# A chunked recurrence with a feed-forward layer: score and state-read products of 64 rows in the two halves of TensorE

## The chip, the cores and the metric

The kernel runs on one core of one Trainium2 chip. The metric is the time of one execution on the device in microseconds (us); the time before is the median of three runs. A core has five engines that run beside each other, each with an instruction queue of its own: TensorE (PE) for matrix products, with a weight load of its own (PEld), VectorE (DVE), ScalarE (ACT), GpSimd (POOL) and SyncE (SP), which in this kernel issues all DMAs. Products land in PSUM, which has banks of 128 partitions x 512 float32; everything else lies in SBUF.

## What is computed

Four sequences (`batch`), 8 heads, 768 tokens, head size D = 32, state size N = 16. For every sequence and head a decaying state of 16 x 32 is carried over the tokens; its output, transposed to tokens x 256, goes through a layer 256 -> 2048 -> 256 with a softplus between.

```python
# per batch and head, chunk by chunk (the kernel takes 128 tokens at a time)
M = (C @ B.T) * decay(i, j)            # "scores", causal
y = M @ x + (C @ state) * decay_to_i   # inside the chunk + "state read"
state = decay_full * state + (B * decay_from_j).T @ x
...
h = y_all @ w_in                       # 3072 x 256 @ 256 x 2048
out = softplus(h) @ w_out              # @ 2048 x 256
```

## The kernel before

**Units.** A unit is 128 tokens of one sequence with all 8 heads: 24 units, 6 to a sequence. Units 0 to 11 (`i < FIRST`) come with C already laid apart by the host; units 12 to 23 come stacked and are made ready on the chip by `split_unit`. The feed-forward layer runs over 6 blocks of 512 tokens (4 units each) and 16 slices of 128 of the inner 2048: `first(j, k)` makes 6 matmuls into a bank `hp`, `parts_of` the softplus and its two roundings (`e`, `gh`, `gl`), `second(j, k)` 6 matmuls into the sums `acc0`, `acc1`. Every factor is split in a high and a low part of type float32r, hence three products for each one. A matmul of plain float32 shows as two instructions in the profile, one of float32r as one.

**Scores.** `score(i, g)` fills one bank `sp` with 4 heads x 128 x 128 (g = 0, 1 for the two groups of four heads). For units under 12 it is one float32 product of 64 rows and 512 columns per group; the two groups lie in rows 0 to 63 and 64 to 127, so each uses one half of the array. From unit 12 on it is two float32r products of 128 rows and 256 columns per group, against `c_rows`, a tile [128, 4, 2, 128] in which the C of two heads is laid apart: rows 0 to 63 of copy e = 0, rows 64 to 127 of copy e = 1, zeros elsewhere. `split_unit` makes the rounded parts of B (`b_rows`) and C (`c_all` for odd units; for even ones the first 512 columns of the constants' tile `kept`, free by then) on ACT and DVE, and two DMAs copy the halves of C into `c_rows`. The word `zero` at the start of the order clears `c_rows` once on POOL. `weigh` multiplies a bank of scores with the decays `rm` on DVE.

**Values and state reads.** Up to unit 7 a unit is read on its own (`read`, `within`, `grow`, `rest`). From unit 8 on units go in pairs. `pair_values(i)` (i even) makes the state products of both units into a bank `zp` (32 columns of the array at a time), the values of both units into one bank `yp` (again 32 columns at a time), and then the state read of unit i into the same bank: `read_into(i, yp)`, two float32 products of 128 rows, 128 columns and 128 tokens, with `tb` (the state spread by `spread`, times a mask `bd` that leaves each head its own rows) and `cc` (scaled C). A unit with i % 6 = 0 has no read. `pair_ends(i)` reads unit i + 1 into that bank, makes `y` = `yp` x `gg` in one DVE instruction of 512 columns, and rounds it to the layer's input (`xh`, `xl`).

**Order.** PE always keeps the order in which the program issues (line 132). Up to step 30 of the layer everything keeps an order written out by hand (`ORDER`, lines 53 to 70); from step 31 (`PINNED`) DVE, ACT and POOL are placed by the scheduler's own cost model. In the main loop a step is `second` of four steps ago, `first`, and then what is planned for it (lines 867 to 875): unit i has its scores in step s = 30 + 4 (i - 12), and for odd i the pair's values in s + 2 and its end in s + 3. So scores stand alone between 6 matmuls `hp` and 6 matmuls `acc`; the read of an odd unit does too; that of an even unit follows the values. Banks of PSUM with the tag `ps` are a ring of six: `hp`, `sp`, `zp` and `yp` take the next in turn, which must have been read out.

Of the kernel before, what the change touches and what calls it, by code (L numbers as in the profile page):

```python
# [10 lines left out]
F32 = mybir.dt.float32  # L11
F32R = mybir.dt.float32r
# [3 lines left out]
ALU = mybir.AluOpType  # L16
PSUM = bass.MemoryType.PSUM

P = 128
NB, NH, S, D, N = 4, 8, 768, 32, 16  # L20
SUB = 32
NC = P // SUB
NU = S // P
NQ = NH // 2
# [4 lines left out]
HEAD = 4  # L29
FIRST = 12  # L30
# [4 lines left out]
U_S = U_C + P  # L35
U_END = U_S + 2 * NQ * P
F_END = U_S + P + NQ * P
# [8 lines left out]
C_SEL = C_BD + NH  # L46
C_GB = C_SEL + P
C_OWN = C_GB + 4
C_END = C_OWN + 2 * NU * (NC + 1)

ORDER = """
zero la warm11 kc un2 hc1 hc0 hc2 un0 logr loga un1 logr loga w2 growth gb hc3 ft0 growth un3 gq0 ft0 w1 B2 D0 un5 fr0
gq0 gq2 fr0 D1 w0 S0 gq2 w7 B0 S1 M0 un6 B1 M0 U0 fr0 M1 D2 I0 fr0 U0 gd M1 C1 S2 T1 un4 D3 W2 G0 un7 U1 C2 M2 U2 R1
B3 G0 W2 ft2 M2 C3 X0 D5 U1 W1 W2 U3 ft2 I1 fr2 warm3 U2 T2 fr2 S5 G1 T3 G1 U3 W2 R2 T4 S3 W2 w3 M5 X1 M5 I2 gg3 W2 R3
D4 M3 fr2 W0 warm6 B4 C4 M3 fr2 U4 C5 W0 warm1 D7 S4 G2 U4 gg6 W0 G2 I3 T5 S6 W0 M4 W0 R5 X2 R4 M4 C7 I5 w4 W0 D6 I4
# [16 lines left out]
LAG = 4  # L74
WRAW = 4
EARLY = 8


def constants():

    k = np.arange(P)
    ch = k // SUB
    upto = (k[:, None] <= k[None, :]).astype(np.float32)
    mid = np.stack([(ch < c) + 0.5 * (ch == c) for c in range(NC)], 1).astype(np.float32)
    out = np.zeros((P, K_END + C_END), np.float32)
    mats = [(mid[:, c : c + 1] - upto) * (ch <= c)[None, :] for c in range(NC)] + [1.0 - upto]
    for i, m in enumerate(mats):
        out[:, i * P : (i + 1) * P] = m
    out[:, C_V : C_V + NC] = mid
    out[:, C_V + NC] = 1.0  # L90
    sel = out[:, K_END:]
    sel[:, C_BD : C_BD + NH] = k[:, None] // N == np.arange(NH)[None, :]
    part = (k // N) % 4
    gb = part >= 2
    gc = part % 2 == 1
    sel[:, C_GB + 0] = gb
    sel[:, C_GB + 1] = 1.0 - 2.0 * gb
    sel[:, C_GB + 2] = gc
    sel[:, C_GB + 3] = 1.0 - 2.0 * gc
    sel[:, C_SEL:C_GB] = (k % NH)[:, None] == (k // N)[None, :]  # L100
    sel[:, C_OWN:] = (k // NH)[:, None] == (np.arange(2 * NU * (NC + 1)) // (NC + 1))[None, :]
    return out


# [1 line left out]
def recurrence_then_ffn(ctx: ExitStack, tc: tile.TileContext, fst, un, alr, w_in, w_out, const, outT):  # L106
# [25 lines left out]
    PE = InOrder(nc.tensor, True)  # L132
# [3 lines left out]
    def load(out, in_):  # L136

        tc.keep_in_program_order(nc.sync.dma_start(out, in_))  # L138
# [107 lines left out]
            gg_s[i + v] = gg[:, :, v * P : v * P + P]  # L246


    c_rows = cp.tile([P, NQ, 2, P], F32R, name="c_rows")

    def split_unit(i):
        if i < FIRST:
            return
        t = bc_s[i]
        b_rows = p2.tile([P, NQ, P], F32R, tag="b_rows", name=f"b_rows{i}")

        def split(out, j):
            raw = t[:, j * NQ * P : (j + 1) * NQ * P].rearrange("p (q t) -> p q t", q=NQ)
            g, be = (kb[:, C_GB + v : C_GB + v + 1] for v in (2 * j, 2 * j + 1))
            A.activation(out, raw, AF.Copy, scale=be)  # L260
            V.scalar_tensor_tensor(out, raw, g, out.bitcast(F32), op0=ALU.mult, op1=ALU.add)

        if i % 2:
            c_all = p2.tile([P, NQ, P], F32R, tag="c_all", name=f"c_all{i}", bufs=1)
        else:
            c_all = kept[:, : NQ * P].bitcast(F32R).rearrange("p (q t) -> p q t", q=NQ)
        split(c_all, 1)
        for e in range(2):
            rows = slice(64 * e, 64 * e + 64)
            load(c_rows[rows, :, e].bitcast(F32), c_all[rows].bitcast(F32))  # L270
        split(b_rows, 0)
        st[i] = b_rows

    some = p2.tile([P, 512], F32, tag="o0", name="some", bufs=1)[:, :16].bitcast(BF16)

# [73 lines left out]
        return xparts[j], t0 - starts[j]  # L349

    bd = kb[:, C_BD : C_BD + NH]
    state = {}

    mid = defaultdict(dict)

    def decays(i):

        b, u = divmod(i, NU)
        fc = f_tok[b][1]
        rm = p2.tile([P, NH, NC, SUB], F32, tag="rm", name=f"rm{i}")  # L360
        Pl.affine_select(  # L361
            out=rm.rearrange("p h c i -> p (h c) i"),
            in_=fc[:, u].rearrange("p h c -> p (h c)").unsqueeze(2).broadcast_to([P, NH * NC, SUB]),
            pattern=[[0, NH], [SUB, NC], [1, SUB]],
            compare_op=ALU.is_ge,
            fill=0.0,
            base=0,
            channel_multiplier=-1,
        )
        mid[i]["rm"] = rm  # L370
# [24 lines left out]

    def score(i, g):
        sp = mid[i]["sp", g] = ps.tile([P, 512], F32, tag="ps", name=f"sp{i}_{g}")
        if i < FIRST:
            rows = slice(64 * g, 64 * g + 64)
            if i < HEAD:  # L400
                t = head_in["l"][rows, i]
                PE.matmul(sp, t[:, :P], t[:, P:], start=True, stop=True)
                return
            PE.matmul(sp, un_s[i][rows, U_S : U_S + P], un_s[i][rows, U_S + P : F_END], start=True, stop=True)
            return
        b_rows = st[i]
        for v in range(2):
            q = 2 * g + v
            PE.matmul(
                sp[:, 2 * v * P : 2 * (v + 1) * P],  # L410
                b_rows[:, q],
                c_rows[:, q].rearrange("p e t -> p (e t)"),
                start=True,
                stop=True,
            )

    def weigh(i, g):
        if g == 0:
# [31 lines left out]
    def spread(i):  # L450

        if i % NU > 0:
            tb = mid[i]["tb"] = p2.tile([P, NQ, 2, D], F32, tag="tb", name=f"tb{i}", bufs=3)
            V.tensor_tensor(
                tb,
                state[i - 1].rearrange("p (e d) -> p e d", d=D).unsqueeze(1).broadcast_to([P, NQ, 2, D]),
                bd.rearrange("p (q e) -> p q e", e=2).unsqueeze(3).broadcast_to([P, NQ, 2, D]),
                op=ALU.mult,
            )

# [41 lines left out]

    def attend_scores(i):
        decays(i)
        for g in range(2):
            score(i, g)
            weigh(i, g)
        scale_b(i)
        scale_c(i)
# [14 lines left out]
    def read_into(i, yp):  # L524
        if i % NU > 0:
            for g in range(2):
                PE.matmul(
                    yp[:, g, i % 2],
                    mid[i]["tb"][:, 2 * g : 2 * g + 2].rearrange("p q e d -> p (q e d)"),
                    mid[i]["cc"].rearrange("p c i -> p (c i)"),  # L530
                    start=False,
                    stop=True,
                    skip_group_check=True,
                )

    def pair_values(i):

        zp = ps.tile([P, 512], F32, tag="ps", name=f"zp{i}")
        for v in range(2):
            if (i + v) % NU < NU - 1:  # L540
                bp = mid[i + v]["bp"]
                for q in range(NQ):
                    PE.matmul(
                        zp[32 * q : 32 * q + 32, 2 * v * D : 2 * (v + 1) * D],
                        bp[:, 2 * q : 2 * q + 2, :].rearrange("p h n -> p (h n)"),
                        un_s[i + v][:, U_X + 2 * q * D : U_X + 2 * (q + 1) * D],
                        start=True,
                        stop=True,
                    )
        mid[i]["zp"] = zp  # L550
        bank = mid[i]["yp"] = ps.tile([P, 512], F32, tag="ps", name=f"yp{i}")
        yp = bank.rearrange("p (g v t) -> p g v t", g=2, v=2)
        for v in range(2):
            m = mid[i + v]["m"]
            for g in range(2):
                for hh in range(4):
                    h = g * 4 + hh
                    PE.matmul(
                        yp[32 * hh : 32 * hh + 32, g, v],
                        un_s[i + v][:, U_X + h * D : U_X + (h + 1) * D],  # L560
                        m[:, h, :],
                        start=v == 0 and g == 0,
                        stop=True,
                        skip_group_check=True,
                    )
        read_into(i, yp)
        yield
        next_state(i, zp)

    def pair_ends(i):  # L570
        yp = mid[i]["yp"].rearrange("p (g v t) -> p g v t", g=2, v=2)
        read_into(i + 1, yp)
        yield
        next_state(i + 1, mid[i]["zp"])
        yield
        y = p2.tile([P, 2, 2 * P], F32, tag="y", name=f"y{i}")
        V.tensor_tensor(y, mid[i]["yp"].rearrange("p (g t) -> p g t", g=2), gg_p[i], op=ALU.mult)
        (xh, xl), c0 = x_parts(i * P)
        hi = xh[:, :, c0 : c0 + 2 * P]
        yield  # L580
        A.copy(hi, y)
        yield
        V.tensor_tensor(xl[:, :, c0 : c0 + 2 * P], y, hi.bitcast(F32), op=ALU.subtract)
        mid.pop(i), mid.pop(i + 1)
# [213 lines left out]
    def both_scores(i):  # L798
# [37 lines left out]
        "E": finish,  # L836
        "v": staged(pair_values),
        "e": staged(pair_ends),
        "zero": lambda: Pl.memset(c_rows.bitcast(F32), 0.0),
    }  # L840
    for word in ORDER.split():
        name = word.rstrip("0123456789.")
# [105 lines left out]
```

## Time and profile before

| | us |
|---|---|
| median of 3 runs (337.09 to 338.31) | 338.07 |
| the profiled execution, its own time | 336.96 |
| its span, first to last instruction | 335.0 |
| PE busy (98% of the span) | 326.9 |
| PEld busy (77%) | 256.8 |
| DVE busy (61%) | 205.6 |
| ACT busy (51%) | 170.9 |

The profile is of one execution; times in it count from the first instruction. A row of the timeline gives start and length of an instruction, or of several alike that follow each other, in us; `128*128` behind a matmul are the rows and columns of the array that it uses, then come the form of the moving tile and the count. "L128" is a helper's line through which most instructions pass, so rows are told apart by their tiles.

### The profile page before, as it was taken

Reading aid. Unit: us, or ns where it says so; the run is one execution under the profiler, and the core shown is the slowest. Engines: PE = TensorE matmul, PEld = TensorE weight load, DVE = VectorE, ACT = ScalarE, POOL = GpSimd, SP = SyncE. Lnnn points to the kernel's source line nnn. Section 1 sums busy time; section 2 is a strip of 40 time slices with the busy share of each in tenths; the row PEclk is TensorE's granted clock in tenths of the full one; section 3 lists DMA queues with packets and bytes.
Section 4 is the critical chain, followed back from the end, with each engine's and each line's share of the span. In section 5 each row is a group of like instructions: output and inputs, shape, how many; then the busy total and the mean of one; then the engine's idle time right before and its main releaser. Section 6 shows DMA issues by size and latency. Waiting matters only on the chain.

```text
span 335.0 us, 5230 instructions
## 1 busy us (share of the span) xinstructions
PE 326.9 (98%) x1990; PEld 256.8 (77%) x1990; DVE 205.6 (61%) x359; ACT 170.9 (51%) x309; POOL 38.0 (11%) x32
## 2 busy tenths in 40 slices
PE   8999899999999999999999999999999999999995
PEld 5545586878867877878888888878888888888885
DVE  2999789999965246687466477478455324322222
ACT  5643666677643446546536446436535425544450
POOL 2632300210011001011011011011010000000000
PEclk9999999999999999999999999999999999999999
DMA  7993756252042015445132353235121000010001
GB/s 267 396 337 111 235 206 213 70 189 63 3 135 86 0 63 154 131 147 147 53 101 77 107 171 102 75 108 138 44 89 33 1 2 0 14 51 0 0 0 64
DMA packets 21848, 35.00 MB, mean 104 GB/s; under 512 B 1856, under 2 KB 11072, under 8 KB 21824
## 3 DMA queue, kind: packets, MB, share of 16 engines
q1 hardware_dynamic: 21824, 34.68, 32.5%
q8 instruction: 15, 0.25, 0.3%
q14 instruction: 9, 0.07, 0.1%
HBM read 28.29 MB, written 3.24 MB: 94 GB/s over the span
## 4 chain that ended last, share of the span: by engine, by line
PE 84%; DMA 7%; DVE 5%; issue 1%; ACT 1%; POOL 1%; SPq 1%; DVEq 0%; ACTq 0%; POOLq 0%
PE acc L128 37%; PE hp L128 36%; PE yp L128 4%; DMA un<-in_fst 4%; PE sp L128 2%; DMA wraw<-in_w_out 2%; DMA un<-in_un 1%; PE warm L128 1%; DVE m L128 1%; PE end L128 1%; PE zp L128 1%; POOL rm L128 1%; DVE w L128 1%; SPq L138 1%; DMA gg<-gd 0%
## 5 line engine op out<-in xcount | busy, mean ns | idle before, releaser
L686 DVE TENSOR_TENSOR gl<-e,gh 128x512 fp32r<-128x512 f32 x65 | 50.8, 786 | 49.6 <-ACT gh L680 48.8
L128 PE MATMUL hp<-xh,wih 128*128 128x512 f32 (+1 forms) x204 | 78.0, 382 | 0.0
L128 PE MATMUL hp<-xh,wil 128*128 128x512 f32 (+1 forms) x204 | 76.9, 377 | 0.5 <-DVE wil L128 0.5
L128 PE MATMUL hp<-xl,wih 128*128 128x512 f32 (+1 forms) x204 | 76.8, 377 | 0.0
L128 PE MATMUL acc<-gh,woh 128*128 128x512 f32 x188 | 75.2, 400 | 0.8 <-DVE half L128 0.8
L128 PE MATMUL acc<-gl,woh 128*128 128x512 f32 x188 | 73.7, 392 | 0.8 <-DVE gl L128 0.8
L674 ACT ACTIVATE e<-hp 128x512 f32<-128x512 f32 x65 | 38.7, 595 | 69.3 <-PE hp L128 68.9
L128 PE MATMUL acc<-gh,wol 128*128 128x512 f32 x188 | 73.3, 390 | 0.0
L128 PEld LDWEIGHTS hp<-xh,wih 128*128 128x128 f32 x204 | 38.3, 188 | 10.2 <-issue 2.3
L128 PEld LDWEIGHTS hp<-xh,wil 128*128 128x128 f32 x204 | 38.3, 188 | 8.0 <-DVE wil L128 0.9
L128 PEld LDWEIGHTS hp<-xl,wih 128*128 128x128 f32 x204 | 38.4, 188 | 7.1
L128 PEld LDWEIGHTS acc<-gh,woh 128*128 128x128 f32 x188 | 35.4, 188 | 10.4 <-ACT e L128 2.0
L680 ACT CAST gh<-e 128x512 fp32r<-128x512 f32 x65 | 40.2, 619 | 5.0 <-PE acc L128 3.4
L128 PEld LDWEIGHTS acc<-gl,woh 128*128 128x128 f32 x188 | 35.4, 188 | 7.7 <-DVE gl L128 1.4
L128 PEld LDWEIGHTS acc<-gh,wol 128*128 128x128 f32 x188 | 35.3, 188 | 7.4
L361 POOL TENSOR_SCALAR_AFFINE_SELECT rm<-fc 128x1024 f32<-128x1024 f32 x11 | 17.0, 1541 | 133.9 <-DVE m L420 95.8
L128 DVE TENSOR_TENSOR gl<-e,gh 128x512 fp32r<-128x512 f32 x31 | 21.2, 684 | 14.0 <-ACT gh L128 14.0
L128 POOL TENSOR_SCALAR_AFFINE_SELECT rm<-fc 128x1024 f32<-128x1024 f32 x13 | 19.6, 1508 | 71.4 <-DVE m L128 48.7
L128 ACT ACTIVATE e<-hp 128x512 f32<-128x512 f32 x31 | 18.4, 594 | 12.3 <-PE hp L128 11.5
L128 ACT CAST gh<-e 128x512 fp32r<-128x512 f32 x31 | 19.1, 619 | 10.0 <-PE acc L128 9.4
L128 DVE SCALAR_TENSOR_TENSOR w<-wraw,w 128x512 int32<-128x512 int32 x32 | 22.7, 725 | 0.1
L128 DVE TENSOR_TENSOR m<-sp,rm 128x512 f32<-128x512 f32 x26 | 17.5, 679 | 0.0
(99 smaller groups left out, 299.8 us busy)
## 6 DMA issues: line engine op xcount, KB each, us to landing
bc<-in_un SPq DMA_DIRECT2D x12, 512.0 KB
un<-in_fst SPq DMA_DIRECT2D x8, 576.0 KB
wraw<-in_w_in SPq DMA_DIRECT2D x8, 512.0 KB
wraw<-in_w_out SPq DMA_DIRECT2D x8, 512.0 KB
un<-in_un SPq DMA_DIRECT2D x12, 256.0 KB
out_t<-o SPq DMA_DIRECT2D x9, 256.0 KB
gg<-gd SPq DMA_DIRECT2D x16, 128.0 KB
c_rows<-kept SPq DMA_DIRECT2D x12, 128.0 KB
```

What stands on the lines that cost most here:

```text
L128: return lambda *a, **k: tc.keep_in_program_order(f(*a, **k))
L138: tc.keep_in_program_order(nc.sync.dma_start(out, in_))
L361: Pl.affine_select(out=rm.rearrange("p h c i -> p (h c) i"), in_=fc[:, u].rearrange("p h c -> p (h c)").unsqueeze(2).broadcast_to([P, NH * ...
L674: A.activation(e, h, AF.Softplus)
L680: A.copy(gh, e)
L686: V.tensor_tensor(gl, e, gh.bitcast(F32), op=ALU.subtract)
```

## The change

The product of a head's scores needs 64 rows only. In `split_unit` the copies into `c_rows` go, and with them the tile, its clearing and the use of `kept`; `c_all` gets two buffers for all units. The host stacks the heads in another order, so that rows 0 to 63 hold heads 0 to 3 and rows 64 to 127 heads 4 to 7. The scores of a unit from 12 on are eight float32r products of 64 rows and 128 columns, in turn in the upper and lower half of the array, each half into its own bank.

```diff
-        for e in range(2):
-            rows = slice(64 * e, 64 * e + 64)
-            load(c_rows[rows, :, e].bitcast(F32), c_all[rows].bitcast(F32))
...
+    def split_scores(i):
+        b_rows, c_all = st[i]
+        for g in range(2):
+            mid[i]["sp", g] = ps.tile([P, 512], F32, tag="ps", name=f"sp{i}_{g}")
+        for q in range(NQ):
+            for g in range(2):
+                rows = slice(64 * g, 64 * g + 64)
+                PE.matmul(
+                    mid[i]["sp", g][:, q * P : q * P + P], b_rows[rows, q], c_all[rows, q], start=True, stop=True
+                )
...
     def attend_scores(i):
         decays(i)
+        split_scores(i)
         for g in range(2):
-            score(i, g)
             weigh(i, g)
```

The state reads from unit 8 on (`PAIRED`) become products of 64 rows too: `tb` is made with a mask `b4` of four columns (new in the constants) and is half as long, and each half of the array reads into a bank of its own, so that a pair's `yp` is two banks instead of one, and `y` two DVE instructions of 256 columns.

```diff
+            n, own = (2, b4) if i >= PAIRED else (NQ, bd)
             V.tensor_tensor(
-                tb,
+                tb[:, :n],
...
     def read_into(i, yp):
         if i % NU > 0:
             for g in range(2):
+                rows = slice(64 * g, 64 * g + 64)
                 PE.matmul(
-                    yp[:, g, i % 2],
-                    mid[i]["tb"][:, 2 * g : 2 * g + 2].rearrange("p q e d -> p (q e d)"),
-                    mid[i]["cc"].rearrange("p c i -> p (c i)"),
+                    yp[g][:, i % 2],
+                    mid[i]["tb"][rows, :2].rearrange("p q e d -> p (q e d)"),
+                    mid[i]["cc"][rows].rearrange("p c i -> p (c i)"),
...
-        bank = mid[i]["yp"] = ps.tile([P, 512], F32, tag="ps", name=f"yp{i}")
-        yp = bank.rearrange("p (g v t) -> p g v t", g=2, v=2)
+        yp = mid[i]["yp"] = [
+            ps.tile([P, 512], F32, tag="ps", name=f"yp{i}_{g}")[:, : 2 * P].rearrange("p (v t) -> p v t", v=2)
+            for g in range(2)
+        ]
...
-        V.tensor_tensor(y, mid[i]["yp"].rearrange("p (g t) -> p g t", g=2), gg_p[i], op=ALU.mult)
+        for g in range(2):
+            V.tensor_tensor(y[:, g], yp[g].rearrange("p v t -> p (v t)"), gg_p[i][:, g], op=ALU.mult)
```

More of the change, by code (lines that the diff above doesn't have):

```diff
@@ L48 @@
 C_OWN = C_GB + 4
-C_END = C_OWN + 2 * NU * (NC + 1)
+C_B4 = C_OWN + 2 * NU * (NC + 1)
+C_END = C_B4 + 4
 ORDER = """
-zero la warm11 kc un2 hc1 hc0 hc2 un0 logr loga un1 logr loga w2 growth gb hc3 ft0 growth un3 gq0 ft0 w1 B2 D0 un5 fr0
+la warm11 kc un2 hc1 hc0 hc2 un0 logr loga un1 logr loga w2 growth gb hc3 ft0 growth un3 gq0 ft0 w1 B2 D0 un5 fr0
 gq0 gq2 fr0 D1 w0 S0 gq2 w7 B0 S1 M0 un6 B1 M0 U0 fr0 M1 D2 I0 fr0 U0 gd M1 C1 S2 T1 un4 D3 W2 G0 un7 U1 C2 M2 U2 R1
@@ L76 @@
 EARLY = 8
+PAIRED = 8
 def constants():
@@ L100, in constants @@
     sel[:, C_SEL:C_GB] = (k % NH)[:, None] == (k // N)[None, :]
-    sel[:, C_OWN:] = (k // NH)[:, None] == (np.arange(2 * NU * (NC + 1)) // (NC + 1))[None, :]
+    sel[:, C_B4:] = (k // N % 4)[:, None] == np.arange(4)[None, :]
+    sel[:, C_OWN:C_B4] = (k // NH)[:, None] == (np.arange(2 * NU * (NC + 1)) // (NC + 1))[None, :]
     return out
@@ L246, in load_growth @@
             gg_s[i + v] = gg[:, :, v * P : v * P + P]
-    c_rows = cp.tile([P, NQ, 2, P], F32R, name="c_rows")
     def split_unit(i):
@@ L261, in split @@
             V.scalar_tensor_tensor(out, raw, g, out.bitcast(F32), op0=ALU.mult, op1=ALU.add)
[L263 to L266, printed above, removed]
+        c_all = p2.tile([P, NQ, P], F32R, tag="c_all", name=f"c_all{i}")
         split(c_all, 1)
-        for e in range(2):
-            rows = slice(64 * e, 64 * e + 64)
-            load(c_rows[rows, :, e].bitcast(F32), c_all[rows].bitcast(F32))
         split(b_rows, 0)
-        st[i] = b_rows
+        st[i] = b_rows, c_all
     some = p2.tile([P, 512], F32, tag="o0", name="some", bufs=1)[:, :16].bitcast(BF16)
@@ L351, in recurrence_then_ffn @@
     bd = kb[:, C_BD : C_BD + NH]
+    b4 = kb[:, C_B4 : C_B4 + 4]
     state = {}
@@ L397, in score @@
         sp = mid[i]["sp", g] = ps.tile([P, 512], F32, tag="ps", name=f"sp{i}_{g}")
[L398 to L404, printed above, removed]
-            return
[L406 to L415, printed above, removed]
+        rows = slice(64 * g, 64 * g + 64)
+        if i < HEAD:
+            t = head_in["l"][rows, i]
+            PE.matmul(sp, t[:, :P], t[:, P:], start=True, stop=True)
+            return
+        PE.matmul(sp, un_s[i][rows, U_S : U_S + P], un_s[i][rows, U_S + P : F_END], start=True, stop=True)
+    def split_scores(i):
[8 more added lines that the diff above has]
+                )
     def weigh(i, g):
@@ L453, in spread @@
             tb = mid[i]["tb"] = p2.tile([P, NQ, 2, D], F32, tag="tb", name=f"tb{i}", bufs=3)
+            n, own = (2, b4) if i >= PAIRED else (NQ, bd)
             V.tensor_tensor(
-                tb,
-                state[i - 1].rearrange("p (e d) -> p e d", d=D).unsqueeze(1).broadcast_to([P, NQ, 2, D]),
-                bd.rearrange("p (q e) -> p q e", e=2).unsqueeze(3).broadcast_to([P, NQ, 2, D]),
+                tb[:, :n],
+                state[i - 1].rearrange("p (e d) -> p e d", d=D).unsqueeze(1).broadcast_to([P, n, 2, D]),
+                own.rearrange("p (q e) -> p q e", e=2).unsqueeze(3).broadcast_to([P, n, 2, D]),
                 op=ALU.mult,
@@ L526, in read_into @@
             for g in range(2):
+                rows = slice(64 * g, 64 * g + 64)
                 PE.matmul(
-                    yp[:, g, i % 2],
-                    mid[i]["tb"][:, 2 * g : 2 * g + 2].rearrange("p q e d -> p (q e d)"),
-                    mid[i]["cc"].rearrange("p c i -> p (c i)"),
+                    yp[g][:, i % 2],
+                    mid[i]["tb"][rows, :2].rearrange("p q e d -> p (q e d)"),
+                    mid[i]["cc"][rows].rearrange("p c i -> p (c i)"),
                     start=False,
@@ L558, in pair_values @@
                     PE.matmul(
-                        yp[32 * hh : 32 * hh + 32, g, v],
+                        yp[g][32 * hh : 32 * hh + 32, v],
                         un_s[i + v][:, U_X + h * D : U_X + (h + 1) * D],
                         m[:, h, :],
-                        start=v == 0 and g == 0,
+                        start=v == 0,
                         stop=True,
@@ L570, in pair_ends @@
     def pair_ends(i):
-        yp = mid[i]["yp"].rearrange("p (g v t) -> p g v t", g=2, v=2)
+        yp = mid[i]["yp"]
         read_into(i + 1, yp)
@@ L838, in recurrence_then_ffn @@
         "e": staged(pair_ends),
-        "zero": lambda: Pl.memset(c_rows.bitcast(F32), 0.0),
     }
@@ L906, in stacked @@
     def stacked(t):
-        v = t.reshape(NB, NQ, 2, NU, P, N).transpose(0, 3, 2, 5, 1, 4)
+        v = t.reshape(NB, 2, NQ, NU, P, N).transpose(0, 3, 1, 5, 2, 4)
         v = np.broadcast_to(v[:, :, :, None], (NB, NU, 2, 4, N, NQ, P))
```

## The prediction

> **What bounds the kernel now.** I read the page first: the busy shares and the chain that ended last. Then the busy time by stretches, then the timeline of PE and PEld around every matmul that the change touches.
>
> ```profile
> span 335.0 us, 5230 instructions
> PE 326.9 (98%) x1990; PEld 256.8 (77%) x1990; DVE 205.6 (61%) x359; ACT 170.9 (51%) x309; POOL 38.0 (11%) x32
> PE 84%; DMA 7%; DVE 5%; issue 1%; ACT 1%; POOL 1%; SPq 1%; DVEq 0%; ACTq 0%; POOLq 0%
> ```
> ```profile
> 50.00:128.00 78.00, 76.30 (x414) 59.23 (x414) 58.92 (x105) 45.02 (x78) 6.78 (x4) 1.00 0.28 90
> 128.00:280.00 152.00, 151.85 (x946) 125.12 (x945) 92.13 (x150) 75.00 (x127) 15.28 (x10) 1.00 0.32 92
> ```
> ```profile
> 143.05 2.72 PE hp L128 x12
> ```
>
> The columns of the stretches are PE, PEld, DVE, ACT and POOL busy, then the granted clock and the DMA's share. All twelve score visits and ten of the fourteen reads that change lie in 128 to 280 us, and there PE is busy 151.85 of 152 us at full clock: no other engine ever holds it up. So whatever the change adds to PE's own time between two ordinary matmuls, or takes from it, arrives in the end. DVE (92 of 152) and the DMA (0.32) are cover. The chain's piece gives the ordinary pitch: 2.72 us for 12 matmuls of 512 columns, 0.227 us each. I price every visit of other matmuls as the time from the last ordinary start before it to the second ordinary start behind it, less two pitches (0.454 us).
>
> **The change part by part.** *Scores, 12 units.* Before, one visit:
>
> ```profile
> 215.77 0.39 PE L128 MATMUL hp<-xh,wil 128*128 128x512 f32 x1
> 216.00 0.64 PE L128 MATMUL sp<-c_rows,b_rows 128*128 128x256 f32 x4
> 216.47 0.40 PE L128 MATMUL acc<-gh,woh 128*128 128x512 f32 x1
> 216.71 0.40 PE L128 MATMUL acc<-gl,woh 128*128 128x512 f32 x1
> ```
>
> 216.71 - 215.77 = 0.94, less 0.454: 0.49 us. The first score starts one pitch behind hp and the first acc follows the fourth score at 0.12: this visit pays nothing at its edges.
>
> No float32r product of 64 rows stands in the trace, but float32 ones do, for units under 12. To read them, first a state read that stands alone, whole array, and the lengths of all reads (shortest, median, longest in ns):
>
> ```profile
> 225.93 0.39 PE L128 MATMUL hp<-xh,wil 128*128 128x512 f32 x1
> 226.16 0.60 PE L128 MATMUL yp<-cc,tb 128*128 128x128 f32 x4
> 226.52 0.48 PE L128 MATMUL acc<-gh,woh 128*128 128x512 f32 x1
> 226.84 0.40 PE L128 MATMUL acc<-gl,woh 128*128 128x512 f32 x1
> ```
> ```profile
> L128 PE MATMUL yp<-cc,tb x80: 270/275/377, 13.7 to 276.7; 128*128 128x128 f32 x80
> ```
>
> Four instructions in 0.60 us, the last 0.275 long: (0.60 - 0.275) / 3 = 0.108 us for a float32 instruction of 128 columns, so 0.43 for one of 512. Now a visit of 64-row scores, as PE and as PEld show it:
>
> ```profile
> 68.39 0.39 PE L128 MATMUL hp<-xh,wil 128*128 128x512 f32 x1
> 68.70 1.13 PE L128 MATMUL sp<-un 64*128 64x512 f32 x4
> 69.76 0.50 PE L128 MATMUL acc<-gh,woh 128*128 128x512 f32 x1
> 70.10 0.39 PE L128 MATMUL acc<-gl,woh 128*128 128x512 f32 x1
> ```
> ```profile
> 68.70 0.18 PEld L128 LDWEIGHTS sp<-un 64*128 64x128 f32 x1 [0.35 <-ACT gh L128]
> ...
> 68.70 0.30 PEld L128 LDWEIGHTS sp<-un 64*128 64x128 f32 x4 [0.35 <-ACT gh L128]
> 69.76 0.19 PEld L128 LDWEIGHTS acc<-gh,woh 128*128 128x128 f32 x1 [0.76 <-DVE half L128]
> 69.87 0.19 PEld L128 LDWEIGHTS acc<-gl,woh 128*128 128x128 f32 x1
> ```
>
> It costs 70.10 - 68.39 - 0.454 = 1.26 us. Its streams, both halves side by side, are two instructions deep: 0.86. The other 0.40 is at the edges, and the rows show where. hp should give way at 68.39 + 0.227 = 68.62; the scores start at 68.70, and their weight load starts there too, not ahead of it as in the visit above. On the way out acc's weight load again starts with its matmul, at 69.76, after 0.76 idle. So **each change between whole array and halves costs about 0.09 us until the array is empty, and then a weight load of 0.11 us that nothing covers** (69.76 to 69.87 is the spacing of two loads). Twice 0.20 is 0.40. The four half loads fit in 0.30 us, the first alone is 0.18 long: two by two, 0.11 apart. A half load thus takes as long as a whole one, only the two halves load together.
>
> After: eight loads and eight products, in four pairs. The products' streams are shorter than the loads: 256 columns of float32r came every 0.12, so 128 take 0.054 at that rate, and at most the 0.108 of a float32 instruction of that width. I take 0.054, since float32r is the row nearest in type. Either way the load's 0.11 sets the pitch: 0.40 at the edges (first load included) + 3 x 0.11 + a last stream of 0.054 = 0.784 us (0.84 with 0.108). That is +0.30 a unit (+0.35): **12 x 0.30 = +3.6 us**. The lower end, edges free, is 0.44 - 0.49 = -0.05 a unit; the upper, two instructions to a product, is rival C.
>
> *The copies into c_rows* hold PE up once, at unit 12:
>
> ```profile
> 126.15 1.38 SPq L138 DMA_DIRECT2D c_rows<-kept  x2
> ```
> ```profile
> 129.03 0.39 PE L128 MATMUL hp<-xh,wil 128*128 128x512 f32 x1
> 129.57 0.71 PE L128 MATMUL sp<-c_rows,b_rows 128*128 128x256 f32 x4
> 130.12 0.39 PE L128 MATMUL acc<-gh,woh 128*128 128x512 f32 x1
> 130.35 0.39 PE L128 MATMUL acc<-gl,woh 128*128 128x512 f32 x1
> ```
>
> 130.35 - 129.03 - 0.454 = 0.87 against 0.49. Nothing but the copies, issued from 126.15 to 127.53, is late there, so **-0.4 us**. The other copies are worth nothing to PE: it does not wait there. On SP's queue the copies go from ahead of the loads of later units, which then leave earlier; what those hide behind is the same full PE.
>
> *Reads alone (odd units 9 to 23: 8).* Before, by the row shown above, 226.84 - 225.93 - 0.454 = 0.46 us. After: the four instructions become two side by side, 2 x 0.108, plus the edges of 0.40: 0.62. +0.16 each, **+1.3 us**; between -0.24 (edges free) and +0.27 if the two halves start one instruction apart.
>
> *Reads behind values (units 8, 10, 14, 16, 20, 22: 6).*
>
> ```profile
> 172.12 1.06 PE L128 MATMUL yp<-m,un 128*32 128x128 f32 x32
> 173.10 0.71 PE L128 MATMUL yp<-cc,tb 128*128 128x128 f32 x4
> 173.57 0.47 PE L128 MATMUL acc<-gh,woh 128*128 128x512 f32 x1
> 173.88 0.39 PE L128 MATMUL acc<-gl,woh 128*128 128x512 f32 x1
> ```
>
> The values work in columns of 32, so the edge into the read is paid already. From 173.10 to the second acc, less one pitch: 0.78 - 0.227 = 0.55 us. After: load 0.11, two instructions 0.216, a second edge 0.20: 0.53. **-0.02 each, -0.1 us.**
>
> *DVE, POOL and banks.*
>
> ```profile
> L454 DVE TENSOR_TENSOR tb<-state,kept 128x256 f32<-128x256 f32 x10 | 4.2, 422 | 0.2
> L128 DVE TENSOR_TENSOR y<-yp,gg 128x256 f32<-128x256 f32 x8 | 3.2, 410 | 0.0
> L577 DVE TENSOR_TENSOR y<-yp,gg 128x512 f32<-128x512 f32 x6 | 4.1, 690 | 7.1 <-PE yp L128 7.1
> 179.42 0.68 DVE L577 TENSOR_TENSOR y<-yp,gg 128x512 f32<-128x512 f32 x1
> 181.46 0.39 PE L128 MATMUL hp<-xh,wih 128*128 128x512 f32 x1
> ```
>
> y in two pieces costs 2 x 410 - 690 = +130 ns a pair, tb of half the length saves some 140 (422 at 256 columns): DVE even, and covered; without that cover it would be a tenth of a microsecond a pair. The cleared tile on POOL lies at the very start, beside loads: nothing. The second yp bank shortens the ring: the hp two steps behind a pair's end now waits for y's first half instead of zp. In the pair quoted that hp starts at 181.46, and y's first half would be done at 179.42 + 0.41 = 179.83: 1.6 us to spare.
>
> **Sum:** 3.6 - 0.4 + 1.3 - 0.1 = **+4.4 us**. On the profiled execution's own time, 336.96, that gives 341.4. That execution was 1.1 us quicker than the median of the runs shown, 338.07; the added time is the same for both, so I forecast 342.5.
>
> **The rivals.** *A. Edges overlap, and the halves pay* (not slower). If the halves' loads ran ahead of the edge and the array did not empty, scores would take 4 x 0.11 = 0.44 (-0.05 x 12), reads alone 0.22 (-0.24 x 8), reads behind values 0.33 (-0.22 x 6), unit 12 -0.4: together -4.2, 333.9 us. It decides as soon as both edges of a score visit come under 0.05 us. Against it stand the 64-row visits of the trace: both edges show, in and out. For it: those are float32, the new ones float32r. The Trainium skill (TensorE: Matmul & The Clock Gate, Part 3, "Measured speedup vs the span model") lets row tiles share a stream for some 4 ns each and measured 3.07x for four of them; the trace agrees on the sharing (four half loads in 0.30 us), not on the edges, which that section does not price. 7%.
>
> *B. Only the emptying is paid.* With 0.09 a side and the loads covered, 0.22 less for each of the 26 visits: 4.4 - 5.7 = -1.3, 336.8 us, no change by measure. Against it: the weight load at 69.76 begins with its matmul. The Trainium skill (TensorEngine Tiling (Array Packing), "Key Properties") says only that changing the mode drains the TensorE; by that rule alone the sum would be this one, and here the rows show more than it says. 8%, with waits that go elsewhere.
>
> *C. Narrow float32r costs double.* If a product of 128 columns ran as two instructions, as float32 does, a pair would take 0.216 and a visit 0.40 + 4 x 0.216 = 1.26: 12 x 0.48 = +5.8 on top, 348.3 us. No row excludes it. 10%.
>
> *D. The bank ring.* If y came over 1.6 us later than now, hp would wait in every pair; one us in each of eight pairs gives 350.5. y stands in DVE's order behind splits that wait for loads, so the slack is not fixed. 5%.
>
> One more piece is loose: the scheduler's placing.
>
> ```profile
> 95.33 4.59 DMA un<-in_un
> ...
> 99.95 0.29 DVE cc L392
> ```
> ```profile
> 100.89 0.43 PE L128 MATMUL yp<-m,un 128*32 128x128 f32 x8 [0.40 <-DVE m L128]
> ```
>
> A cc was placed on DVE ahead of unit 11's second weighing and waited for its load; PE then waited 0.40 us in the values of pair 10. A new program can lose that or gain another: +-1 us in the forecast's own range.
>
> **How the numbers follow.** Forecast 70% (342.5, own range 340.8 to 344.5: +-1 of placing, 0.6 for the last stream, 0.9 for halves out of step in the reads), A 7, B 8, C 10, D 5. The range leaves out A, B's lower part, C's and D's far ends: 339.5 to 346.0. Half a percent, 1.7 us, is about what a measurement of this kernel can tell from no change. Slower: the forecast, C and D, less one in a hundred for placing that eats the loss, 0.84; same: that one and B, 0.09; faster: A, 0.07.
>
> **What would show it.** Of the changed kernel: a score visit of eight `64*128` matmuls with its weight load starting with the first of them, a gap of about 0.09 us ahead, acc's load uncovered behind it, near 0.78 us by the same rule; the read alone near 0.62; sixteen score instructions a unit instead of eight mean C; PE idle before hp with y as releaser means D; a visit under 0.49 us means A. The forecast is wrong if the edges are not there, or if PE has new waits in 128 to 280 us.

## The result and the profile after

| | before | after |
|---|---|---|
| median of 4 runs, us | 337.97 (337.09 to 338.31) | 342.57 (342.31 to 343.32) |
| profiled execution, own time, us | 336.96 | 342.34 |
| its span, us | 335.0 | 340.5 |

The ratio is 1.0144, 95% interval 1.0118 to 1.0170: the changed kernel is slower by 4.6 us. The forecast was 342.5. All ratios, here and below, leave out runs more than 1.5% above the quickest of their kernel; there was one, of 341.76 us, in the last experiment.

From the page after, span and busy shares; and the busy time by stretches (the columns as in the prediction):

```profile
span 340.5 us, 5282 instructions
PE 332.6 (98%) x2038; PEld 254.5 (75%) x2038; DVE 201.3 (59%) x367; ACT 172.9 (51%) x309; POOL 37.1 (11%) x31
```
```profile
128.00:283.00 155.00, 155.00 (x987) 121.81 (x986) 86.63 (x154) 76.55 (x127) 15.24 (x10) 1.00 0.22 69
```

PE has 48 matmuls more (12 units with eight score products instead of four) and is busy in all of 155 us: it is still the one bound, and no new wait took the stretch. PEld is busy less although it has 48 loads more, because the loads of the two halves run side by side: the 48 loads of the scores kept it busy for 7.3 us, the 96 now do for 6.2. DVE and the DMA (0.22 for 0.32) have less to do, and nothing came of it.

The timeline of PE around one score visit, one read alone and one read behind values, for the changed kernel:

```profile
167.73 0.39 PE L131 MATMUL hp<-xh,wil 128*128 128x512 f32 x1
168.05 0.66 PE L131 MATMUL sp<-c_all,b_rows 64*128 64x128 f32 x8
168.65 0.49 PE L131 MATMUL acc<-gh,woh 128*128 128x512 f32 x1
168.98 0.39 PE L131 MATMUL acc<-gl,woh 128*128 128x512 f32 x1
...
178.61 0.39 PE L131 MATMUL hp<-xh,wil 128*128 128x512 f32 x1
178.93 0.49 PE L131 MATMUL yp<-cc,tb 64*128 64x128 f32 x4
179.35 0.50 PE L131 MATMUL acc<-gh,woh 128*128 128x512 f32 x1
179.69 0.39 PE L131 MATMUL acc<-gl,woh 128*128 128x512 f32 x1
...
175.56 0.49 PE L131 MATMUL yp<-cc,tb 64*128 64x128 f32 x4
175.98 0.50 PE L131 MATMUL acc<-gh,woh 128*128 128x512 f32 x1
176.32 0.39 PE L131 MATMUL acc<-gl,woh 128*128 128x512 f32 x1
```

By the prediction's rule (less two pitches of 0.227): the score visit is 168.98 - 167.73 - 0.454 = 0.80 us (0.49 before), the read alone 179.69 - 178.61 - 0.454 = 0.63 (0.46), the read behind values 176.32 - 175.56 - 0.227 = 0.53 (0.55). Both edges stand in the score visit: hp gives way at 167.73 + 0.227 = 167.96 and the scores start at 168.05. The timeline of PEld there:

```profile
167.51 0.19 PEld L131 LDWEIGHTS hp<-xh,wil 128*128 128x128 f32 x1
168.05 0.52 PEld L131 LDWEIGHTS sp<-c_all,b_rows 64*128 64x128 f32 x8 [0.35 <-issue]
168.65 0.19 PEld L131 LDWEIGHTS acc<-gh,woh 128*128 128x128 f32 x1
168.75 0.19 PEld L131 LDWEIGHTS acc<-gl,woh 128*128 128x128 f32 x1
```

For 0.35 us ahead of the scores no weights are loaded, and acc's load starts with acc, at 168.65. "issue" means that the load waited for nothing that the profile shows, so no operand is seen to be late. Eight loads in 0.52 us, 0.19 long: (0.52 - 0.19) / 3 = 0.11 from pair to pair.

Unit 12's score visit, which had waited for the copies:

```profile
130.45 0.39 PE L131 MATMUL hp<-xh,wil 128*128 128x512 f32 x1
130.77 0.66 PE L131 MATMUL sp<-c_all,b_rows 64*128 64x128 f32 x8
131.36 0.49 PE L131 MATMUL acc<-gh,woh 128*128 128x512 f32 x1
131.69 0.39 PE L131 MATMUL acc<-gl,woh 128*128 128x512 f32 x1
```

131.69 - 130.45 - 0.454 = 0.79: it is like the others now, the wait has gone.

The two spans differ by 5.5 us, the medians by 4.6. The rest lies ahead of the change: unit 9's scores, which the change doesn't touch, start at 68.70 in the profile before and at 69.61 in the one after. That is ordinary spread: in the profiles of the experiments that follow, the repeat of the kernel before left out, they start anywhere from 68.61 to 70.87.

### The profile page after: what moved, and what is told of

Its sections match the earlier page's. It is cut to its first block, busy times and chain, and to the rows that moved or that the text cites. A ratio compares the mean times of both kernels' runs of the same rounds, so it can differ in the third digit from the quotient of the medians.

```text
span 340.5 us, 5282 instructions
## 1 busy us (share of the span) xinstructions
PE 332.6 (98%) x2038; PEld 254.5 (75%) x2038; DVE 201.3 (59%) x367; ACT 172.9 (51%) x309; POOL 37.1 (11%) x31
## 4 chain that ended last, share of the span: by engine, by line
PE 83%; DMA 7%; DVE 5%; issue 1%; SPq 1%; POOL 1%; ACT 0%; DVEq 0%; ACTq 0%; POOLq 0%
PE acc L131 38%; PE hp L131 35%; PE yp L131 4%; DMA un<-in_fst 3%; PE sp L131 3%; DMA wraw<-in_w_out 2%; PE warm L131 1%; DVE m L131 1%; DMA un<-in_un 1%; SPq L141 1%; DVE y L131 1%; PE end L131 1%; DVE w L131 1%; PE zp L131 1%; POOL rm L131 1%
## 5 line engine op out<-in xcount | busy, mean ns | idle before, releaser
L686 DVE TENSOR_TENSOR gl<-e,gh 128x512 fp32r<-128x512 f32 x65 | 44.7, 690 | 58.1 <-ACT gh L680 57.6
L131 PE MATMUL acc<-gh,woh 128*128 128x512 f32 x188 | 76.6, 408 | 0.8 <-DVE half L131 0.8
L131 DVE TENSOR_TENSOR gl<-e,gh 128x512 fp32r<-128x512 f32 x31 | 21.3, 687 | 16.0 <-ACT gh L131 15.9
L415 DVE TENSOR_TENSOR m<-sp,rm 128x512 f32<-128x512 f32 x22 | 14.2, 686 | 15.7 <-PE sp L131 15.7
```

The source lines that it names most:

```text
L131: return lambda *a, **k: tc.keep_in_program_order(f(*a, **k))
L415: V.tensor_tensor(mid[i]["m"][:, 4 * g : 4 * g + 4].rearrange("p h t -> p (h t)"), mid[i].pop(("sp", g)), mid[i]["rm"][:, 4 * g : 4 * g + ...
L686: V.tensor_tensor(gl, e, gh.bitcast(F32), op=ALU.subtract)
```

## The experiments

The theory is that of the prediction: every change of the array between whole and halves costs PE some 0.20 us, in which the array empties and a weight load stands uncovered, and inside a visit a pair of half products comes as often as a weight load takes, 0.11 us. The rivals stand with each run. All ratios are to the kernel before, on the same chip. Experiments of a single run show how long a visit is; their total can be off by the 1 to 3 us that runs of one kernel differ by.

**Scores alone** (the changed `split_unit` and scores; reads, `yp` and `y` as before). Against the kernel before:

```diff
+        split_scores(i)
         for g in range(2):
-            score(i, g)
             weigh(i, g)
```

> Only the scores part of the change; state reads, yp and y as before. Edge theory (each change between whole array and halves costs PE some 0.20 us, and pairs come at the pitch of a weight load, 0.11): a score visit of 0.79 us instead of 0.48, unit 12's wait of 0.38 gone, in all 12 x 0.31 - 0.4 = +3.3 us, 341.3. Rival (the loss comes from the second yp bank, the two pieces of y or other waits): score visits may be longer, but the total stays within 1 us of before, 338 to 339.

Ratio 1.0075 (1.0048 to 1.0101): +0.75%, 2.5 us, where 3.3 were expected (inside the interval, which reaches 3.4). Between the two profiles, counted from unit 9's scores on, it is (338.4 - 68.86) - (335.0 - 68.70) = 3.2. A score visit, from its timeline:

```profile
166.41 0.39 PE L128 MATMUL hp<-xh,wil 128*128 128x512 f32 x1
166.73 0.66 PE L128 MATMUL sp<-c_all,b_rows 64*128 64x128 f32 x8
167.32 0.49 PE L128 MATMUL acc<-gh,woh 128*128 128x512 f32 x1
167.66 0.39 PE L128 MATMUL acc<-gl,woh 128*128 128x512 f32 x1
```

167.66 - 166.41 - 0.454 = 0.80, as in the whole change: more than half of the loss is here, without the second bank.

**Reads alone** (`tb`, `read_into`, two `yp` banks and `y` in two pieces as changed; scores from `c_rows`). Against the changed kernel:

```diff
-        split_scores(i)
         for g in range(2):
+            score(i, g)
             weigh(i, g)
```

> Only the reads part: reads of 64 rows from unit 8 on, two yp banks, y in two pieces; scores and the copies of C as before. Edge theory: 8 reads alone at 0.62 instead of 0.45, 6 behind values 0.02 shorter, +1.3 us, 339.3; score visits stay at 0.48 and unit 12's at 0.86. Rival (second bank, pieces of y, other waits carry the loss): +3 us or more, 341, with hp waiting for y.

Ratio 1.0045 (1.0021 to 1.0068): +0.45%, 1.5 us. The read alone takes 180.30 - 179.22 - 0.454 = 0.63:

```profile
179.22 0.39 PE L131 MATMUL hp<-xh,wil 128*128 128x512 f32 x1
179.54 0.49 PE L131 MATMUL yp<-cc,tb 64*128 64x128 f32 x4
179.97 0.50 PE L131 MATMUL acc<-gh,woh 128*128 128x512 f32 x1
180.30 0.39 PE L131 MATMUL acc<-gl,woh 128*128 128x512 f32 x1
```

The two parts add up to 1.20% for the whole's 1.44%, within their intervals of about a quarter of a percent each. Neither part needs the other for its loss. `y` isn't among the causes of PE's waits in this profile, so the rival falls.

**Half the columns.**

```diff
-                    mid[i]["sp", g][:, q * P : q * P + P], b_rows[rows, q], c_all[rows, q], start=True, stop=True
+                    mid[i]["sp", g][:, q * P : q * P + 64], b_rows[rows, q], c_all[rows, q, :64], start=True, stop=True
```

> The changed kernel with scores of units 12 to 23 for the first 64 tokens alone (64 columns stream instead of 128), used for the other 64 too; this leaves out half of those products, and weighing is four DVE instructions. Load theory (the pitch of a pair is its weight load, 0.11 us): a score visit falls by one narrower last stream only, 0.79 to 0.76 us. Rival (the pitch is the stream of narrow float32r products): pairs come at 0.06 or less, the visit falls to 0.60 us or less, 2.3 us in all.

In a single run 342.29 us. A visit:

```profile
167.89 0.39 PE L131 MATMUL hp<-xh,wil 128*128 128x512 f32 x1
168.21 0.63 PE L131 MATMUL sp<-c_all,b_rows 64*128 64x64 f32 x8
168.77 0.50 PE L131 MATMUL acc<-gh,woh 128*128 128x512 f32 x1
169.11 0.39 PE L131 MATMUL acc<-gl,woh 128*128 128x512 f32 x1
```

169.11 - 167.89 - 0.454 = 0.77. Half the stream takes 0.03 off the visit, about one narrower last stream. So the pitch is not the stream's; it is that of the weight loads, 0.11. A limit on how fast PE can start instructions doesn't explain it: eight products here are 0.055 us apart on average, while the prediction's row at 172.12 has 32 products, each on 32 columns of the array, in 1.06 us, 0.03 each.

**One half after the other.**

```diff
-        for q in range(NQ):
-            for g in range(2):
+        for g in range(2):
+            for q in range(NQ):
```

> The changed kernel with the eight score products in another order: first four in the upper half, then four in the lower. If two products run at once only because they alternate, and a half load takes as long as a whole one: eight loads one behind another, 0.40 + 7 x 0.11 + 0.05 = 1.2 us a visit instead of 0.79, +5 us in all, 347.5. Rival (each half works off its own queue): the visit stays at 0.79 and the time at 342.6.

In a single run 341.99 us. I expected 1.2 us a visit and was wrong; the rival gave the right one:

```profile
167.21 0.39 PE L131 MATMUL hp<-xh,wil 128*128 128x512 f32 x1
167.53 0.67 PE L131 MATMUL sp<-c_all,b_rows 64*128 64x128 f32 x8
168.13 0.50 PE L131 MATMUL acc<-gh,woh 128*128 128x512 f32 x1
168.47 0.39 PE L131 MATMUL acc<-gl,woh 128*128 128x512 f32 x1
```

168.47 - 167.21 - 0.454 = 0.81. Eight loads one behind another would take 0.11 x 8 = 0.9 and the eight products could not fit in 0.67. So the second half's products must start while some of the four of the first half, which stand ahead of them in the program, have not (the rows don't name the half; this is inferred from the time). Alternating them by hand is worth 0.01 us.

**Two visits of four.**

```diff
+        plan(s + 1, attend_rest, i)      # the products q = 2, 3, then both weighings
```

> The changed kernel with each unit's eight score products in two visits of four, one step apart, weighing after the second. Edge theory: each visit costs 0.40 at its edges whatever it holds, so two of 0.40 + 0.11 + 0.05 = 0.57 us instead of one of 0.79, +0.34 x 12 = +4.1 us, 346.7. Rival (the 64-row products are slow in themselves, edges are cheap): two of 0.40, the total unchanged at 342.6.

In a single run 346.08 us, 3.5 more than the changed kernel's median, and the first of unit 15's two visits starts like this:

```profile
168.28 0.39 PE L131 MATMUL hp<-xh,wil 128*128 128x512 f32 x1
168.59 0.44 PE L131 MATMUL sp<-c_all,b_rows 64*128 64x128 f32 x4
168.96 0.50 PE L131 MATMUL acc<-gh,woh 128*128 128x512 f32 x1
169.30 0.39 PE L131 MATMUL acc<-gl,woh 128*128 128x512 f32 x1
```

169.30 - 168.28 - 0.454 = 0.57, as expected. From 168.59 to acc's start four products take 0.37 us, eight in the changed kernel 0.60 (168.05 to 168.65): halving the work saves 0.23, two loads' pitch, and the rest is paid again with each visit. That is the edge theory from the other side: same products, twelve visits more, and the time moves by about 0.3 us for each. Between this profile and the changed kernel's, counted from unit 9's scores on, it is (344.1 - 68.90) - (340.5 - 69.61) = 4.3 us, where 4.1 were expected.

**Merged reads.** The read of the odd unit goes into the visit of the even one, where an edge is paid anyhow.

```diff
         mid[i]["zp"] = zp
+        next_state(i, zp)
...
         read_into(i, yp)
+        read_into(i + 1, yp)
         yield
-        next_state(i, zp)
```

> The changed kernel with the odd unit's read moved into the same visit as the even unit's, behind the pair's values, and the even unit's new state made ahead of the values. Edge theory: eight reads alone (0.62 each) go, each adds 0.22 to the visit behind the values, and the two pairs whose even unit has no read (12 and 18) pay an edge more, 0.2: -8 x 0.40 + 2 x 0.2 = -2.8 us, 339.7. Rival (a read's cost is its products): no gain, 342.6. A third way: tb comes late from DVE and PE waits in the visit, which gives some of it back.

Ratio 1.0136 (1.0112 to 1.0159), 343.27 on 338.0: no gain on the changed kernel's 1.0144. The visits of pairs 8, 14, 16, 18 and 22, in which PE doesn't wait, came out as the edge theory has them; that of pair 20 saved only 0.09, and that of pair 12, which waits 0.46 us for `tb`, lost 0.32. Pair 14:

```profile
179.07 0.71 PE L131 MATMUL yp<-cc,tb 64*128 64x128 f32 x8
179.71 0.50 PE L131 MATMUL acc<-gh,woh 128*128 128x512 f32 x1
180.05 0.39 PE L131 MATMUL acc<-gl,woh 128*128 128x512 f32 x1
```

180.05 - 179.07 - 0.227 = 0.75 for both reads, where the changed kernel pays 0.53 + 0.63: 0.40 saved, one pair of edges. The third way then took it back, in the values of pair 10:

```profile
102.93 0.43 PE L131 MATMUL yp<-m,un 128*32 128x128 f32 x8 [0.84 <-DVE m L131]
103.29 0.49 PE L131 MATMUL yp<-cc,tb 64*128 64x128 f32 x4
104.80 0.49 PE L131 MATMUL yp<-cc,tb 64*128 64x128 f32 x4 [1.02 <-DVE tb L131]
...
105.79 0.63 PE L131 MATMUL hp<-xl,wih 128*128 128x512 f32 x1
106.22 0.63 PE L131 MATMUL hp<-xh,wil 128*128 128x512 f32 x1
```
```profile
105.00:108.00 3.00, 3.00 (x11) 2.30 (x10) 0.76 (x2) 0.00 (x0) 0.00 (x0) 0.55 0.02 5
```

PE waits 0.84 for the weighing and 1.02 for `tb`, and behind these waits the granted clock is 0.55 for 3 us: hp comes every 0.43 us (105.79 to 106.22) instead of 0.227. So 3.00 x 0.45 = 1.35 us are lost on top of the 1.9 us of waits. The Trainium skill (TensorE: Matmul & The Clock Gate, Part 1, "What's actually happening") says that an activity monitor halves TensorE's clock when TensorE has been idle for a window of some 3.4 us. The trace agrees on the halving (0.55), but not on the whole window: from 100 to 105 us PE was busy for 3.14 of 5 us. The mean clock of this whole execution is 0.995, and three of the four runs have that; the fourth, at 1.00, took 341.79, still over the 339.7 expected.

**Merged reads, old scores.** The same with `score` from `c_rows`, so that only the reads differ from the kernel before.

> The same merged reads of 64 rows, but scores of 128 rows against C laid apart, as in the kernel before. Edge theory: halves pay where an edge is paid anyway (reads, one edge out of the values) and lose where the visit stands alone (scores). From the last run's 339.7: -12 x 0.31 + 0.4 = -3.4, 336.3 us, about 0.5% faster than the kernel before. Rival (halves lose everywhere): 339 or more.

Ratio 1.0049 (1.0024 to 1.0074), 339.51 on 338.0, runs from 337.44 to 342.36. Better than the whole change by about the scores' part, but not the 336.3 that I expected, and no better than the reads alone unmerged (1.0045): pair 10 waits as above in its profile too, 0.9 us at the longest for the weighing and 1.0 for `tb`. But that profile is of the quickest run, and its clock stays full through that stretch (1.00, third from the right):

```profile
50.00:128.00 78.00, 75.04 (x412) 58.10 (x411) 58.58 (x107) 43.89 (x76) 6.78 (x4) 1.00 0.27 90
```

So waits of this length don't halve the clock every time. Of the twelve runs the three with a mean clock of 0.999 or more took 337.44 to 339.07, the nine with 0.989 to 0.995 took 339.06 to 342.36.

**The hand-written order four steps longer.**

```diff
-PINNED = 31
+PINNED = 35
```

> As the run before, with the hand-written order of DVE, ACT and POOL kept for four steps more (PINNED 35 instead of 31), so that unit 13's cc isn't placed ahead of unit 11's weighing. If the wait of PE in the values of pair 10 comes from that placing, that visit falls back to some 1.75 us plus the merged read, and 0.4 to 1.0 us of the total with it, 335.5. If not, the visit stays as long as in the run before.

Ratio 1.0063 (1.0041 to 1.0086), 340.7 on 338.0, where 335.5 was expected. Pair 10's wait has gone, but the long wait moved on: in the waits of PE, longest on the right, it is now the read of pair 12 that waits, 1.9 us in one piece, where it had waited 0.5 in the run before:

```profile
PE yp L131 <- DVE tb L459: 1.9, 1, 1.9
```

Seven of these ten runs have a mean clock of 0.995 or less. Together that makes 19 of the 26 runs with all reads merged; of the 23 runs of the kernel before beside them it is three. A mean doesn't say where the clock fell; in the profile with the wait of 1.9 us it is 0.99 over 128 to 280 us and 1.00 ahead of that.

**The kernel before, once more.**

> The kernel before, unchanged, profiled once more, to see how much two executions of one program differ ahead of the changed stretch. If the 0.9 us by which the changed kernel's profile was late at unit 9's scores (69.61 against 68.70) is the spread of loads at the start, this profile has that visit anywhere within 1 to 2 us of 68.70, and the same visits behind it as in the first profile, but for the wait in pair 10.

In a single run 343.03 us, while 23 other runs of the same kernel beside it lay between 336.86 and 339.72, so this execution was an unusual one. Busy time by stretches:

```profile
0.00:50.00 50.00, 44.57 (x343) 27.23 (x344) 35.56 (x76) 23.73 (x61) 15.96 (x18) 0.93 0.68 236
...
128.00:280.00 152.00, 151.73 (x941) 125.11 (x942) 93.01 (x152) 76.19 (x128) 15.29 (x10) 1.00 0.33 96
```

The first 50 us have a mean clock of 0.93, which costs 50 x 0.07 = 3.5 us, and unit 9's scores start at 73.51 instead of 68.70. That is more than the 1 to 2 us I had allowed, and by itself a run like this doesn't show what the ordinary spread is; the other profiles, 68.61 to 70.87, do. What it adds is that the stretch that the change touches stays the same even here (PE 151.73 busy, 151.85 in the first profile; a score visit costs the same to 0.01). Pair 10's values waited 1.0 us for the weighing instead of 0.4.

**Merging only where it doesn't wait:** scores as before, merged reads of 64 rows in the pairs 8 and 14 to 22, pairs 10 and 12 as before.

```diff
+TOGETHER = (8, 14, 16, 18, 20, 22)
...
+                half = i - i % 2 in TOGETHER
+                rows = slice(64 * g, 64 * g + 64) if half else slice(0, P)
```

> Scores as before; merged reads of 64 rows only in the pairs where the run with all pairs merged showed no long wait (8 and 14 to 22), pairs 10 and 12 as in the kernel before. Edge theory: pairs 8, 14, 16, 22 save 0.25 each, 20 between -0.25 and +0.06, 18 0.03: -1.0 us, 337.0 on 338.0, 0.3% faster, with no half clock. Rival (waits and half clock come with the merged order wherever it is): 339 or more, as with all pairs merged.

> The same with the hand-written order kept for four steps more. If the wait in pair 10's values is the placing of unit 13's cc, that visit falls to 1.77 us from 2.4 or more: 0.6 us or more below the run without, 336.4, 0.5% faster than the kernel before. If the longer order only moves a wait to pair 12, no gain.

Without the longer order the ratio is 0.9964 (0.9943 to 0.9986), 337.38 on 338.11; with it 0.9978 (0.9960 to 0.9996), 337.12. Both are a little faster than the kernel before, and the edge theory's 0.3% is inside both intervals. In both profiles the state products, values and both reads of pair 14 cost 2.08 us by the prediction's rule; before, all but the odd unit's read cost 1.88 and that read 0.45: 0.25 saved, as expected. Merging reads of the whole array was not run; as the whole-array read alone pays no edge (0.45 for four instructions of 0.108), I estimate that it would save next to nothing, so the gain is that of the halves. The longer order does what was expected in pair 10, where PE had waited 1.30 us for the weighing in the first of the two profiles:

```profile
101.45 0.43 PE L131 MATMUL yp<-m,un 128*32 128x128 f32 x8 [1.30 <-DVE m L131]
```
```profile
100.73 1.06 PE L131 MATMUL yp<-m,un 128*32 128x128 f32 x32
```

In the second the 32 value matmuls run through in 1.06 us. But the totals of the two can't be told apart, so the 0.6 us expected between them isn't shown, and the 0.5% expected of the second is outside its interval.

## Why the prediction was right

- **Scores.** Forecast 0.784 a visit and +0.30 a unit; measured 0.80 and +0.31. The price came from float32 visits of another width, and it held because it lies at the edges, which don't depend on what is inside: two visits of four products show that directly, and half the columns show that the stream, the one number without a row, matters by 0.03 us at most. (The prediction's 0.054 for it should have been 0.06, half of the 0.12 it names; that moves the visit by 0.006.) That the 0.09 us of each edge is the array emptying is a reading of the gap; no run takes it apart.
- **The copies.** Unit 12's 0.4 us came back as forecast. That the other copies were worth nothing was not run by itself; the sum has no room for much more.
- **Reads alone.** Forecast 0.62, measured 0.63. The allowance for halves out of step (+0.27 a read instead of +0.16) wasn't needed: the two halves start side by side.
- **Reads behind values.** Forecast 0.53, measured 0.53. Pair 10 is the exception: its whole visit grew from 2.37 to 2.55 us, with the same 0.4 us of waiting in two pieces instead of one.
- **The sum.** +4.4 forecast, +4.6 between the medians. Between the two profiles, counted from unit 9's scores on, it is (340.5 - 69.61) - (335.0 - 68.70) = 4.6 too. The mechanism and its terms are confirmed; that the median met the forecast within 0.1 us is luck, since the runs after spread over 1 us and the sum was 0.2 short.
- **The rivals.** A (edges overlap) and B (only the emptying is paid) fall with the PEld rows: no load ahead of an edge, 0.35 us without any. C (float32r of 128 columns in two instructions) falls with eight matmuls a unit. D (the bank ring) falls with the waits of PE after, where `y` doesn't occur; the two longest:

```profile
PE yp L131 <- DVE m L131: 1.0, 4, 0.3
PE warm L131 <- POOL some L131: 1.0, 1, 1.0
```

- **What was only part right.** The loose piece, the scheduler's placing, was taken as +-1 us. In the change itself pair 10's values waited 0.22 + 0.17 instead of 0.40. With merged reads it was worth more: nearly 2 us of waits in one pair, and a lower mean clock in most runs.

## What to carry to other kernels

Splitting TensorE into halves was priced here by the visit, not by the product: about 0.40 us for going in and out between whole-array matmuls, against 0.23 us for four more score products. It paid only where an edge was paid already (the reads behind the values), and not where weight loads set the pitch, because a load of 64 rows took as long as one of 128. Before rows are halved, look in the weight loads' timeline for whether the visit in question runs without a gap today, and when products are moved together to share an edge, look for which engine then has to be ready earlier.

## What the runs showed of the hardware

- The halves of the array don't keep the program's order between them, as inferred from the time: with four products of one half ahead of four of the other, all eight took 0.67 us, as if they had alternated (0.66). The Trainium skill (TensorE: Matmul & The Clock Gate, Part 3, "The mechanism") has matmuls start and end strictly in order; for products in different halves this run shows otherwise.
- Weight loads didn't run ahead over a change between whole array and halves, in either direction: 0.35 us without a load ahead of the scores, and acc's load starting with acc.
- Waits of PE of 0.84 and 1.02 us, with work between them, were followed by about 3 us of half clock in one execution (0.55 granted from 105 to 108 us), and waits of 0.9 and 1.0 at the same place left it at 1.00 in another. Such waits make the half clock likely, not certain: 19 of 26 runs had a mean clock of 0.995 or less, against three of 23 before.
